# One evacuation for both halves of an attention block, in a fused attention and two-MLP kernel

## The chip, the core and the metric

The kernel runs on one core of a Trainium2 chip. The metric is the device time of one execution in microseconds. Before the change it is 1192.57 us, the median of three runs (1190.59 to 1194.06).

## The reference, cut to what matters

Three stages follow each other. The first is chunked attention: batch 4, 8 heads, 768 positions, head size 64. Each chunk of 32 queries sees 16 positions to its left, itself, 8 to its right, and 8 memory slots.

```python
for c in range(nc):
    scores = scale * np.matmul(q_c, k_full.transpose(0, 1, 3, 2))
    scores = scores - np.max(scores, axis=-1, keepdims=True)
    a = np.exp(scores)
    a = a / (np.sum(a, axis=-1, keepdims=True) + 1e-09)
    out[:, :, c_start:c_end] = np.matmul(a, v_full)
...
h = x @ w_in;  g = np.maximum(h, 0.0) + alpha * np.minimum(h, 0.0);  y = g @ w_out
h = y @ w_in;  g = h * (1.0 / (1.0 + np.exp(-1.702 * h)));           z = g @ w_out
```

The attention result, 3072 tokens by 512 channels, goes through a first MLP (hidden size 2048, leaky activation with a slope per channel) and a second one (gated by a sigmoid). The change lies in the last line of the attention loop: how the product with `v_full` leaves the accumulator.

## The kernel before, in words

The tokens are cut into 12 blocks of 256 (`TB`), numbered `nb`. A block's attention is done in two halves of 128 tokens. All products are made of pairs of 16-bit numbers: a float32 value is split into a rounded high part and a low remainder, and three products stand for one.

**Order of the work.** The first MLP is a loop of 96 steps of a block and a pair of hidden tiles (`order`, L970), 8 steps to a block. In a step `s` (L995) the TensorE does `mlp_g1` of block step `s - 4` (24 matmuls, L575) and later `mlp_g2` of an earlier one (24 matmuls, L655). The ScalarE and the VectorE do the activation (`mlp_act`, L610 and L613) and the split into high and low parts (`mlp_split`, by `cast_hi` L127 and `sub_lo` L130) between them. Three calls of `run_plan` in each step emit whatever else is due: attention of later blocks, the unpacking of weights, the preparation of the second MLP. A unit with time `t` is emitted by the first `run_plan` whose argument is over `t`; `run_plan(3 * s + 1)` stands behind `mlp_g1`, `run_plan(3 * s + 2)` ahead of `mlp_g2`, `run_plan(3 * s + 3)` behind it. The units of the blocks 3 to 11 come from the list `ATT` (L836), with `24 * nb + EX3 - 38` added, where `EX3` is 12; those of blocks 0 to 2 stand in the list `start` (L855). The order of emission is a priority: the kernel is built with `schedule_with_timeline_sim=True` (L1074), and an engine's final order can differ from it. Each engine then works through its own queue in order.

**The end of a block's attention.** For each half `i`, the normalised scores are split (`att_a16`, ScalarE L523, GpSimd L524) and transposed by a DMA that SyncE issues (`att_ta`, L530) into `aT`. `att_pv` (L533) then makes 48 small matmuls of 32 columns (L543: 4 pairs of heads, 4 chunks, 3 products) with the stationary tile `vbd`. Half 0 goes to the first bank of the accumulator tile `sps`, half 1 to the second:

```python
xp = sps[:, i].rearrange("p (j t) -> p j t", j=HP)
```

`sps` has three banks of 512 columns and one copy; the scores `q k` of every half (`att_qk`, L477 and L478) are written to the same tile. `att_xhi` (ScalarE, 512 columns, through L127) rounds a half to 16 bits into `xt`, and `att_xlo` (VectorE, 512 columns, through L130) writes the remainder. `xt` of a block is what its eight `mlp_g1` read.

By the list, the units of a block are emitted in this order: `att_pv` of half 0 at 32 behind the `mlp_g1` of a step; `att_xhi` of half 0 at 33 ahead of that step's `mlp_g2`; `att_xlo` of half 0 and `att_pv` of half 1 at 34 behind it; `att_xhi` and `att_xlo` of half 1 at 35 and 36, in the next step. Two steps after the first product the block's own `mlp_g1` begin. Blocks 0 and 1 use a version in 32 bits (`att_pv32`) with its own accumulator, and are not touched by the change except for a condition that falls away.

Of the kernel before, what the change touches and what calls it, by code (L numbers as in the profile page):

```python
# [26 lines left out]
F32B = (0, 1)  # L27
# [9 lines left out]
def kernel(  # L37
# [23 lines left out]
    HP = H // 2  # L61
# [7 lines left out]
    AS = 2.0 ** 14  # L69
# [56 lines left out]
    def cast_hi(hi, src, s):  # L126
        return nc.scalar.activation(out=hi, in_=src, func=ACTF.Copy, scale=s)  # L127

    def sub_lo(lo, hi, src, s):
        return nc.vector.scalar_tensor_tensor(out=lo, in0=src, scalar=s, in1=hi, op0=ALU.mult, op1=ALU.subtract)  # L130
# [142 lines left out]
    att = {}  # L273
# [8 lines left out]
    def bs(nb, i):  # L282
        return blk[nb][:, i:i + 1]
# [249 lines left out]
    def att_pv(nb, i):  # L533
        aT = att.pop(("a", nb, i))
        if i == 0:
            xt[nb] = xt_p.tile([128, 2, KT, TB], F16, tag="xt", name="xt")
        xp = sps[:, i].rearrange("p (j t) -> p j t", j=HP)
        for j in range(HP):
            for c in range(4):
                o = xp[:, j, 32 * c:32 * c + 32]  # L540
                w = vbd[:, 4 * i + c, j].rearrange("p a (d t) -> p (a d) t", t=2)
                for n, (wt, a) in enumerate(((0, 0), (1, 0), (0, 1))):
                    nc.tensor.matmul(out=o, lhsT=w[:, :, wt], rhs=aT[:, a, j, 32 * c:32 * c + 32], start=(n == 0), stop=(n == 2))  # L543
        att["xp", nb, i] = xp

    def att_xhi(nb, i):
        cast_hi(xt[nb][:, 0, :, i * 128:(i + 1) * 128], att["xp", nb, i], bs(nb, 9) if nb in F32B else 1.0 / AS)

    def att_xlo(nb, i):
        x = xt[nb][:, :, :, i * 128:(i + 1) * 128]  # L550
        sub_lo(x[:, 1], x[:, 0], att.pop(("xp", nb, i)), bs(nb, 9) if nb in F32B else 1.0 / AS)


    xt = {}
# [272 lines left out]
    def run_plan(t):  # L827
# [14 lines left out]
        (18, att_qk, 0), (18, att_ext, 0), (20, att_smax, 0), (21, att_qk, 1), (21, att_ext, 1),  # L842
        (22, att_exp, 0), (23, att_smax, 1), (24, att_sum, 0), (25, att_exp, 1), (26, att_a16, 0),
        (27, att_sum, 1), (28, att_ta, 0), (29, att_a16, 1), (31, att_ta, 1),
        (32, att_pv, 0), (33, att_xhi, 0), (34, att_xlo, 0), (34, att_pv, 1), (35, att_xhi, 1), (36, att_xlo, 1),
    ]
    for nb in range(3, NB):
        for u in ATT:
# [2 lines left out]
    def split(m, p):  # L851
# [16 lines left out]
        (-16.05, w_max, 1, 3), (-15.51, w_max, 0, 3), (-14.02, att_xmax, 0, 0), (-13.25, att_load, 2, 2),  # L868
        (-13.14, att_v32, 1, 0), (-12.97, w_all, 0, 2, 4), (-11.75, w_load, 0, 5), (-11.41, att_xall, 0),
        (-10.4, att_xs, 0), (-9.99, w_scale, 0, 2, 4), (-9.05, att_xhi, 0, 0), (-8.93, att_xlo, 0, 0),  # L870
        (-8.73, w_split_b, 0, 0), (-8.71, att_load, 2, 1), (-8.25, att_xhi, 0, 1), (-7.99, att_load, 2, 0),
        (-7.61, w_dec_a, 0, 2), (-7.5, w_dec_b, 0, 2), (-7.25, w_dec_b, 0, 1), (-7.2, w_load, 1, 5),
        (-6.9, w_max, 0, 4), (-6.52, att_max, 2, 0), (-6.51, att_xlo, 0, 1), (-5.97, w_max, 1, 1),
        (-5.96, att_qk32, 1, 0), (-4.67, w_split_a, 0, 1), (-4.66, w_max, 1, 0), (-3.68, att_max, 2, 2),
        (-2.76, att_max, 2, 1), (-2.32, w_dec_a, 0, 3), (-2.14, w_split_a, 0, 2), (-1.65, w_split_b, 0, 1),
# [22 lines left out]
        (25.09, att_vr, 2, 2), (25.62, w_split_b, 1, 0), (26.74, att_ta, 2, 0), (26.89, w_scale, 0, 6, 8),  # L898
        (27.59, att_a16, 2, 1), (28.18, w_load, 1, 4), (29.46, w_max, 1, 4), (29.5, w_split_a, 0, 4),
        (29.59, att_pv, 2, 0), (30.52, w_scale, 1, 4, 6), (30.65, att_ta, 2, 1), (31.18, w_dec_a, 0, 7),  # L900
        (31.7, w_split_b, 1, 2), (31.87, att_xhi, 2, 0), (32.19, att_pv, 2, 1), (33.03, w_dec_a, 0, 6),
        (33.15, w_split_b, 0, 4), (33.67, w_dec_b, 0, 7), (33.84, w_dec_b, 0, 6), (34.16, att_xhi, 2, 1),
        (34.77, w_split_a, 0, 6), (35.75, att_xlo, 2, 1), (35.88, att_xlo, 2, 0), (36.25, w_dec_b, 0, 5),
        (36.83, w_dec_a, 1, 4), (38.19, w_split_b, 0, 6), (38.37, w_dec_a, 1, 5), (39.13, w_split_a, 0, 5),
        (39.77, w_dec_b, 1, 4), (40.15, w_load, 1, 6), (40.17, w_max, 1, 6), (41.35, w_scale, 1, 6, 8),
        (42.12, w_dec_b, 1, 5), (42.5, w_part, 1), (42.81, w_split_a, 1, 5), (43.12, w_split_b, 0, 5),
# [7 lines left out]
    for g in range(NP):  # L914
        m, p = 2 + g % 2, g // 2
        t = 24 * (g + 3) - 8 + EX3
# [12 lines left out]
    for b in range(NB):  # L929
        t = 3 * ((NP * (b + 1) if b >= NA else HF * (NA + b + 1)) + L0) + 2 - 3  # L930
# [7 lines left out]
    for sb in range(NB // 2):  # L938
        t = Q0 + 48 * sb
# [3 lines left out]
        t = 48 * sb + 80 if sb else 101.5  # L943
# [3 lines left out]
        if sb == NB // 2 - 1:  # L947
            t = Q0 + 20
# [17 lines left out]
    sps = ps_s.tile([128, 3, 512], F32, name="sps")  # L966
# [56 lines left out]
    for q in range(STEPS // 2 + LQ):  # L1023
        t = Q0 + 6 * q
# [19 lines left out]
        if xs:  # L1044
            sb, p = divmod(q, NP)
# [33 lines left out]
```

## Time and profile before

| what | value |
| --- | --- |
| profiled execution, device time | 1190.76 us |
| its span, first to last instruction | 1189.0 us |
| runs | 1190.59, 1192.57, 1194.06 us |
| TensorE busy | 1078.8 us, 91% of the span |
| VectorE busy | 854.6 us, 72% |
| ScalarE busy | 632.8 us, 53% |
| GpSimd busy | 637.4 us, 54% |
| mean granted TensorE clock | 0.954 |

The first MLP with the attention and the weight work takes about the first 740 us, the second MLP the rest. Busy shares are means over the whole span. A time in a view is counted from the span's start. In a line of the timeline the first number is the start, the second the duration, the brackets hold the idle time before it and what ended that; an instruction that follows another closely may begin before the other has ended.

### The profile page before, as it was taken

The numbers are of one execution on the slowest core, as the hardware profiler recorded it, in microseconds if no ns is written. First come the engines' busy times: TensorE is split into PE (matmuls) and PEld (weight loads), VectorE is DVE, ScalarE is ACT, GpSimd is POOL, SyncE is SP. The second block draws the span as 40 slices with busy tenths as digits, with TensorE's granted clock in tenths as the row PEclk, the third lists the DMA queues.
The fourth block names the chain that finished last, engine by engine and source line by source line (L and its number), as shares of the span: only waits on it lengthen the run. The fifth ranks groups of instructions, "written<-read, shape, count | busy, mean of one in ns | idle before, by whom it ended". The sixth has DMA issues, their size and how long they took to land.

```text
span 1189.0 us, 25654 instructions
## 1 busy us (share of the span) xinstructions
PE 1078.8 (91%) x10294; PEld 956.7 (80%) x10294; DVE 854.6 (72%) x1509; ACT 632.8 (53%) x968; POOL 637.4 (54%) x740
## 2 busy tenths in 40 slices
PE   3676779988999887999899999989999999999998
PEld 3665668877888776887788988878888888888887
DVE  6898985659787777858698634787676767667662
ACT  4567555556766475756665632545444444443442
POOL 1244542318756456617562811787685676666672
PEclk8678889999899999999899999999999999999999
DMA  9969227576989678887965390640110202000001
GB/s 207 305 126 192 90 72 160 91 145 181 238 207 262 137 203 164 235 156 191 186 191 139 102 351 19 266 169 19 56 44 6 76 19 80 21 6 14 19 19 37
DMA packets 250536, 154.53 MB, mean 130 GB/s; under 512 B 201200, under 2 KB 221680, under 8 KB 249392
## 3 DMA queue, kind: packets, MB, share of 16 engines
q1 hardware_dynamic: 250416, 152.88, 50.3%
q8 instruction: 81, 1.33, 0.5%
q14 instruction: 39, 0.32, 0.1%
HBM read 91.96 MB, written 38.93 MB: 110 GB/s over the span
## 4 chain that ended last, share of the span: by engine, by line
PE 51%; DVE 19%; DMA 11%; POOL 5%; issue 5%; ACT 4%; SPq 4%; ACTq 0%; DVEq 0%; POOLq 0%
PE acc L669 17%; PE x L586 16%; PE h L575 8%; PE acc L655 8%; DVE g L130 3%; DVE gf L613 2%; DMA q<-q 2%; POOL ga L620 2%; DMA wbig<-in_moe_w_in_dram 2%; DVE wr L198 1%; DVE wmax L124 1%; DMA w<-in_moe_w_in_dram 1%; DVE wr L199 1%; DVE blk L124 1%; DMA vbd<-in_v_dram 1%
## 5 line engine op out<-in xcount | busy, mean ns | idle before, releaser
L620 POOL TENSOR_TENSOR ga<-ga 128x128 f32<-128x128 f32 x384 | 213.1, 579 | 170.7 <-DVE ga L618 158.6
L575 PE MATMUL h<-xt,wbig 128*128 128x256 f16 x2304 | 279.6, 279 | 22.8 <-ACT xt L127 17.0
L655 PE MATMUL acc<-g,wbig 128*128 128x256 f16 x2304 | 280.5, 280 | 8.9 <-DVE yf L685 4.0
L575 PEld LDWEIGHTS <-wbig 128*128 128x128 f16 x2304 | 230.4, 100 | 55.4 <-issue 24.5
L655 PEld LDWEIGHTS <-wbig 128*128 128x128 f16 x2304 | 229.7, 100 | 41.5 <-issue 8.9
L669 PE MATMUL acc<-w2o,g 128*128 128x256 f16 x2016 | 231.7, 274 | 4.0 <-ACT g L127 3.6
L586 PE MATMUL x<-yt,w2i 128*128 128x256 f16 x2016 | 229.9, 273 | 1.0 <-DVE ha L596 0.9
L669 PEld LDWEIGHTS <-g 128*128 128x128 f16 x2016 | 197.7, 98 | 28.9 <-ACT g L127 4.5
L586 PEld LDWEIGHTS <-w2i 128*128 128x128 f16 x2016 | 197.3, 98 | 24.2 <-issue 1.4
L130 DVE SCALAR_TENSOR_TENSOR g<-ga,gk,g 128x896 f16<-128x896 f32 x96 | 121.0, 1266 | 91.2 <-ACT g L127 90.9
L127 ACT ACTIVATE g<-ga,gk 128x896 f16<-128x896 f32 x96 | 99.0, 1038 | 96.0 <-POOL ga L620 87.0
L613 DVE SCALAR_TENSOR_TENSOR gf<-t,oma,h 128x256 f32<-128x256 f32 x192 | 83.5, 473 | 76.9 <-ACT t L610 76.9
L130 DVE SCALAR_TENSOR_TENSOR g<-gf,gk,g 128x512 f16<-128x512 f32 x81 | 80.5, 994 | 20.2 <-ACT g L127 20.0
L610 ACT ACTIVATE t<-h 128x512 f32<-128x512 f32 x96 | 56.7, 591 | 70.0 <-PE h L575 46.3
L803 POOL TENSOR_TENSOR o<-o 128x256 f32<-128x256 f32 x77 | 74.3, 979 | 10.0 <-ACT o L798 9.5
L617 ACT ACTIVATE ga<-ha,l2t 128x512 f32<-128x512 f32 x48 | 34.5, 718 | 80.7 <-DVE ha L598 80.7
L228 POOL TENSOR_TENSOR wt<-wr 128x512 f32<-128x512 f32 x16 | 24.0, 1499 | 81.1 <-DVE wr L205 81.0
L214 POOL TENSOR_TENSOR wbig<-wr,wbig 128x1024 f16<-128x1024 f32 x16 | 35.1, 2202 | 53.4 <-ACT wbig L209 53.4
L127 ACT ACTIVATE g<-gf,gk 128x512 f16<-128x512 f32 x81 | 57.7, 712 | 0.5 <-DVE gf L613 0.4
L494 ACT COPY sc<-sps 32x504 f32<-32x504 f32 (+2 forms) x112 | 56.2, 502 | 1.0
L618 DVE SCALAR_TENSOR_TENSOR ga<-ga,ha 128x512 f32<-128x512 f32 x48 | 35.6, 741 | 21.0 <-ACT ga L617 21.0
L543 PE MATMUL sps<-aT,vbd 128*128 128x32 f16 x960 | 27.5, 179 | 22.7 <-DVE xt L130 16.3
(194 smaller groups left out, 1514.7 us busy)
## 6 DMA issues: line engine op xcount, KB each, us to landing
yt_dr<-yh SPq DMA_DIRECT2D x42, 256.0 KB
yt<-yt_dr SPq DMA_DIRECT2D x42, 256.0 KB
w<-in_moe_w_in_dram SPq DMA_DIRECT2D x10, 1024.0 KB
w<-in_moe_w_out_dram SPq DMA_DIRECT2D x10, 1024.0 KB
vbd<-v_dr SPq DMA_DIRECT2D x80, 112.0 KB
w2i_dr<-wh SPq DMA_DIRECT2D x28, 256.0 KB
w2o_dr<-wh SPq DMA_DIRECT2D x28, 256.0 KB
w2i<-w2i_dr SPq DMA_DIRECT2D x4, 1792.0 KB
```

The source lines that it names most:

```text
L127: return nc.scalar.activation(out=hi, in_=src, func=ACTF.Copy, scale=s)
L130: return nc.vector.scalar_tensor_tensor(out=lo, in0=src, scalar=s, in1=hi, op0=ALU.mult, op1=ALU.subtract)
L494: nc.scalar.copy(d[32 * c:32 * c + 32, ..., 0:WIN], x[32 * c:32 * c + 32, ..., bo + CH * c:bo + CH * c + WIN])
L575: nc.tensor.matmul(out=hp[:, e], lhsT=w[:, wt, o:o + 128], rhs=x[:, xh, kk], start=(n == 0), stop=(n == 3 * KT - 1))
L586: nc.tensor.matmul(out=xs[bank][:, i], lhsT=w[:, o, wt, kk * 256 + c:kk * 256 + c + 128], rhs=yt[sb, yi][:, yh, kk], start=(n == 0), stop= ...
L610: nc.scalar.activation(out=t, in_=hp, func=ACTF.Relu, scale=-1.0)
L613: nc.vector.scalar_tensor_tensor(out=g[:, e], in0=t[:, e], scalar=oma[:, f:f + 1], in1=hp[:, e], op0=ALU.mult, op1=ALU.add)
L618: nc.vector.scalar_tensor_tensor(out=t, in0=t, scalar=1.0, in1=hp, op0=ALU.add, op1=ALU.mult)
L620: nc.gpsimd.tensor_tensor(out=g[:, out_], in0=g[:, x], in1=g[:, y], op=op)
L655: nc.tensor.matmul(out=acc[layer, b][dt // 2][:, dt % 2 * TB:(dt % 2 + 1) * TB], lhsT=w[:, wt, dt * 128:(dt + 1) * 128], rhs=g16[:, gh, e] ...
L669: nc.tensor.matmul(out=acc[layer, b][bank][:, i * 256:(i + 1) * 256], lhsT=g16[:, gh, gs], rhs=w[:, o, wt, p % 2], start=(p == 0 and n == ...
L803: e.tensor_tensor(out=ov[:, out_], in0=ov[:, x], in1=ov[:, y], op=op)
```

## The change

Both halves are multiplied first. The accumulator is laid out anew: a pair of heads now has 256 columns side by side, half 0 in the first 128, half 1 in the others, so that the two banks together hold the block's result in the order in which `xt` wants it. One ScalarE and one VectorE instruction of 1024 columns then take it out. In the list of the later blocks the second product is due at 33.5 and the evacuation at 34; in the list of the start the evacuation of block 2 is due at 35.75. `att_xhi` and `att_xlo` stay for blocks 0 and 1 alone.

```diff
-        xp = sps[:, i].rearrange("p (j t) -> p j t", j=HP)
+        xp = sps[:, 0:2].rearrange("p a (b t) -> p (a b) t", b=2)[:, :, i * 128:(i + 1) * 128]
...
-        att["xp", nb, i] = xp
+
+    def xp_both(nb):
+        return sps[:, 0:2].rearrange("p a n -> p (a n)"), xt[nb].rearrange("p a j t -> p a (j t)")
+
+    def att_x(nb):
+        xp, x = xp_both(nb)
+        cast_hi(x[:, 0], xp, 1.0 / AS)
+        sub_lo(x[:, 1], x[:, 0], xp, 1.0 / AS)
...
-        (32, att_pv, 0), (33, att_xhi, 0), (34, att_xlo, 0), (34, att_pv, 1), (35, att_xhi, 1), (36, att_xlo, 1),
+        (32, att_pv, 0), (33.5, att_pv, 1), (34, att_x),
...
-        (31.7, w_split_b, 1, 2), (31.87, att_xhi, 2, 0), (32.19, att_pv, 2, 1), (33.03, w_dec_a, 0, 6),
-        (33.15, w_split_b, 0, 4), (33.67, w_dec_b, 0, 7), (33.84, w_dec_b, 0, 6), (34.16, att_xhi, 2, 1),
-        (34.77, w_split_a, 0, 6), (35.75, att_xlo, 2, 1), (35.88, att_xlo, 2, 0), (36.25, w_dec_b, 0, 5),
+        (31.7, w_split_b, 1, 2), (32.19, att_pv, 2, 1), (33.03, w_dec_a, 0, 6),
+        (33.15, w_split_b, 0, 4), (33.67, w_dec_b, 0, 7), (33.84, w_dec_b, 0, 6),
+        (34.77, w_split_a, 0, 6), (35.75, att_x, 2), (36.25, w_dec_b, 0, 5),
```

## Rows read from the trace of the kernel before

**Rows 1.** Stretches: us, busy us (instructions) of PE, PEld, DVE, ACT, POOL, clock, DMA

```profile
233.00:673.00 440.00, 399.86 (x4200) 354.37 (x4197) 335.63 (x605) 273.37 (x430) 241.56 (x194) 0.96 0.78 184
```

**Rows 2.** Waits of the TensorE, 225 to 700 us: total, times, longest

```profile
PE sps L543 <- DVE xt L130: 16.3, 5, 4.1
PE sps L477 <- ACT sc L494: 7.2, 4, 2.4
PE sps L543 <- DMA aT<-a: 5.7, 2, 4.6
...
PE h L575 <- ACT xt L127: 3.7, 2, 2.1
```

**Rows 3.** Timelines of TensorE and VectorE, block 10

```profile
621.74 1.35 PE L543 MATMUL sps<-aT,vbd 128*128 128x32 f16 x48
...
629.56 1.44 PE L543 MATMUL sps<-aT,vbd 128*128 128x32 f16 x48 [2.63 <-DVE xt L130]
...
628.82 0.68 DVE L130 SCALAR_TENSOR_TENSOR xt<-sps,xt 128x512 f16<-128x512 f32 x1
```

**Rows 4.** Timelines of ScalarE and TensorE, block 7, its second half

```profile
473.32 1.48 ACT L326 ACTIVATE junk<-kf 128x1536 f16<-128x1536 f32 x1 [3.33 <-DMA kf<-in_mem_k_dram]
...
474.81 0.58 ACT L127 ACTIVATE xt<-sps 128x512 f16<-128x512 f32 x1
...
475.44 1.54 PE L575 MATMUL h<-xt,wbig 128*128 128x256 f16 x8 [2.12 <-ACT xt L127]
```

**Rows 5.** Stretches behind four of these waits, columns as in rows 1

```profile
465.80:470.00 4.20, 4.15 (x67) 3.49 (x67) 0.87 (x2) 3.78 (x5) 4.20 (x5) 0.62 1.24 180
...
475.40:481.50 6.10, 6.07 (x41) 4.80 (x41) 3.79 (x14) 5.46 (x9) 3.74 (x4) 0.72 1.09 270
...
576.20:581.50 5.30, 5.23 (x67) 4.04 (x67) 1.92 (x4) 3.82 (x5) 5.30 (x6) 0.50 1.12 203
...
629.50:633.40 3.90, 3.84 (x63) 3.22 (x63) 0.69 (x2) 0.60 (x1) 0.00 (x0) 0.57 0.73 135
```

**Rows 6.** Timelines of TensorE and of SyncE's transposes, blocks 4, 6 and 8

```profile
288.23 1.35 PE L543 MATMUL sps<-aT,vbd 128*128 128x32 f16 x48
...
296.10 1.23 SPq L530 DMA_TRANSPOSE aT<-a  x1
...
299.42 1.46 PE L543 MATMUL sps<-aT,vbd 128*128 128x32 f16 x48 [4.58 <-DMA aT<-a]
...
397.09 1.35 PE L543 MATMUL sps<-aT,vbd 128*128 128x32 f16 x48
...
401.80 1.29 SPq L530 DMA_TRANSPOSE aT<-a  x1
...
406.21 1.35 PE L543 MATMUL sps<-aT,vbd 128*128 128x32 f16 x48 [3.94 <-DVE xt L130]
...
511.43 1.35 PE L543 MATMUL sps<-aT,vbd 128*128 128x32 f16 x48
...
514.30 1.30 SPq L530 DMA_TRANSPOSE aT<-a  x1
...
517.73 1.37 PE L543 MATMUL sps<-aT,vbd 128*128 128x32 f16 x48 [1.12 <-DMA aT<-a]
```

**Rows 7.** Groups of ScalarE and VectorE, 225 to 700 us: busy, mean ns, idle before

```profile
L127 ACT ACTIVATE xt<-sps 128x512 f16<-128x512 f32 x18 | 10.6, 588 | 14.4 <-PE sps L543 14.4
...
L130 DVE SCALAR_TENSOR_TENSOR xt<-sps,xt 128x512 f16<-128x512 f32 x18 | 12.3, 686 | 19.5 <-ACT xt L127 19.5
```

**Rows 8.** The chain that ended last, 540 to 760 us: start, us, what

```profile
628.90 0.61 DVE xt L130
629.56 1.44 PE sps L543 x48
...
739.52 4.60 PE acc L655 x42
```

**Rows 9.** The same chain, 225 to 480 us, shares of the stretch

```profile
by line: issue 13.0%; DMA q<-q 6.4%; PE h L575 5.6%; DVE g L130 5.1%; DVE gf L613 4.6%; PE acc L655 3.4%; DMA w<-in_moe_w_in_dram 3.3%; DMA qf<-in_q_dram 3.2%; DVE blk L124 3.1%; DVE wmax L124 2.7%; DVE q L130 2.5%; ACT k L127 2.5%; DMA kf<
```

More of the change, by code (lines that the diff above doesn't have):

```diff
@@ L543, in att_pv @@
                     nc.tensor.matmul(out=o, lhsT=w[:, :, wt], rhs=aT[:, a, j, 32 * c:32 * c + 32], start=(n == 0), stop=(n == 2))
-        att["xp", nb, i] = xp
+    def xp_both(nb):
[4 more added lines that the diff above has]
+        sub_lo(x[:, 1], x[:, 0], xp, 1.0 / AS)
     def att_xhi(nb, i):
-        cast_hi(xt[nb][:, 0, :, i * 128:(i + 1) * 128], att["xp", nb, i], bs(nb, 9) if nb in F32B else 1.0 / AS)
+        cast_hi(xt[nb][:, 0, :, i * 128:(i + 1) * 128], att["xp", nb, i], bs(nb, 9))
     def att_xlo(nb, i):
         x = xt[nb][:, :, :, i * 128:(i + 1) * 128]
-        sub_lo(x[:, 1], x[:, 0], att.pop(("xp", nb, i)), bs(nb, 9) if nb in F32B else 1.0 / AS)
+        sub_lo(x[:, 1], x[:, 0], att.pop(("xp", nb, i)), bs(nb, 9))
     xt = {}
```

## The prediction, made before the changed kernel was run

> **What bounds the kernel now.** I looked first at the stretch that holds the blocks 3 to 11, since the edit touches nothing else but block 2. The TensorE is busy for 399.9 of its 440 us, the VectorE for 335.6, the ScalarE and the GpSimd for less [rows 1]: the TensorE is the fullest engine, and about 40 us of it lie idle. Next I asked what ended that idle time. The largest entry is the line that the change edits: five times the second product, L543, waits for the VectorE's remainder `xt` L130, 16.3 us in all [rows 2]. Only half 0 has been evacuated at that point, and half 1 goes to another bank, so no data call for this wait; it is there because both halves share the tile `sps`. The timeline of block 10 shows it from close by: half 0 is multiplied at 621.74, the TensorE goes on with other work, then stands for 2.63 us, up to 629.56, until the VectorE has read half 0 (628.82 + 0.68) [rows 3]. Then I followed the chain of waits, to see where such a wait sets the end. In block 10 it does: the chain goes from that `xt` into the second product [rows 8], and on through the TensorE alone to 744 us, where its last piece of the first MLP ends [rows 8]. Between 225 and 480 us the chain is mostly elsewhere: the two large matmul lines have 5.6% and 3.4% of it, transposes, loads, VectorE work and issue time the rest [rows 9].
>
> **The change part by part.** The sum is made against the profiled execution, 1190.76 us (span 1189.0). It is 1.81 us under the median of 1192.57; I give the time for the median.
>
> *The wait on the first half's evacuation goes.* The second product no longer follows a reader of `sps` from its own block. Of the 16.3 us [rows 2] I leave block 6's 3.94 in, because there its transposed `aT` comes hardly earlier (below) [rows 6]: 12.4 us of TensorE idle time go, in the blocks 5, 7, 9 and 10.
>
> *The late second evacuation goes.* In block 7 the first `mlp_g1` of the block waits 2.12 us for half 1's `xt`, which stood in the ScalarE's queue behind an instruction that waited 3.33 us for a load of the next block [rows 4]. Two such waits cost 3.7 us [rows 2]. The single evacuation is emitted a step earlier, ahead of that instruction, so I count them as gone.
>
> *The clock behind these waits.* After four of them the granted clock is 0.62, 0.72, 0.50 and 0.57 for 4.2, 6.1, 5.3 and 3.9 us [rows 5]. A stretch at mean clock c loses (1 - c) of its length: 1.6 + 1.7 + 2.7 + 1.7 = 7.6 us. If the waits go, so does this.
>
> *The second product comes earlier in its queue, and may meet its own DMA.* Now it is emitted ahead of the step's `mlp_g2`, not behind it. What is late next is `aT`. In block 4 the transpose is issued at 296.10 and the product starts at 299.42, 3.3 us on; in block 8 it is 3.4 us [rows 6]; for block 6, issued at 401.80, that makes an estimate of 405.2. If the second product stood directly behind the first, it would wait there from the first one's end: block 4 from 289.6 to 299.4, block 6 from 398.4 to 405.2, block 8 from 512.8 to 517.7. That is 9.8 + 6.8 + 4.9 = 21.5 us where 4.58 + 3.94 + 1.12 = 9.6 are waited now [rows 6], a loss of 11.9. If the builder keeps it where it stands, behind the `mlp_g2`, the loss is 0. These are the bounds; I take the middle, 6.0, since nothing in the trace tells the new place. In the other blocks `aT` was there, or the wait would be named for it.
>
> *The evacuation itself.* No row shows 1024 columns out of `sps`. A gain is bounded by the instruction that goes: ScalarE between 588 and 1176 ns, VectorE between 686 and 1372 ns [rows 7]; a cost above two of the old ones is excluded because no work is added. The elements are the same, so I take something near the upper end, some 0.1 us saved on each engine and block: 0 on the path. What covers it is the TensorE, busier than both. If that cover is gone, ten blocks give back 2 us at most.
>
> *The wait for both halves.* From the end of the second product to a finished `xt` it was 588 + 686 ns; it becomes at most 1176 + 1372, 1.3 us more. Behind the waiting ScalarE instruction stand the same step's activation L610 and, later, the rounding of the next block's `v`; behind the VectorE's stand L613 and the remainder of the `v` part. The ScalarE waits for `sps` now as well, 14.4 us in all, and the VectorE 19.5 us for the ScalarE's `xt` [rows 7]; these two waits become one of each per block. I count 0, because the block's own `mlp_g1` is emitted two steps after, and a step takes 7.0 us (511.43 less 288.23, for the 32 steps from block 4 to block 8 [rows 6]). Without that cover it costs ten times 1.3 us, 13 us.
>
> *The rest.* Matmuls, their order in a bank and the DMAs are the same in number; nothing moves past SyncE or GpSimd work. In block 2 the roundings move behind a weight rounding, while the remainders were the last to come; I take 0, within one of the old instructions, 0.7 us, either way [rows 7].
>
> **Sum.** On the TensorE's queue: 12.4 + 3.7 + 7.6 - 6.0 = 17.7 us. How much of it reaches the end? Certain places are where the chain passes: block 10, 2.63 + 1.7 = 4.3 us [rows 3, 5, 8]; and block 7's first `mlp_g1`, 2.12 + 1.7 = 3.8 us [rows 4, 5], less half of block 8's possible loss, (4.9 - 1.12) / 2 = 1.9 [rows 6]. That makes 6.2. Of the other 11.5 I give a sixth, 1.9, since the chain before is mostly not the TensorE's [rows 9]. Forecast: 8 us less, **1184.5 us**.
>
> A rule of the Trainium skill speaks against the edit: Perfetto Trace Analysis, section Optimizing Tensor Performance, asks that independent groups rotate through PSUM banks so that the evacuation of one overlaps the next group's matmuls. The trace agrees with the aim but shows that this overlap does not happen in five of the blocks, where the next group starts only when the evacuation is over [rows 2, 3]. By the rule the sum would be a loss, by the rows it is the gain above.
>
> **The rivals.**
>
> *Absorbed.* The waits go, but other queues hold the pace, and the TensorE waits elsewhere: for `sc` L494 before the scores, 7.2 us now [rows 2], or for `aT`. For it speaks the chain of 225 to 480 us [rows 9]; against it block 10, behind which the chain knows the TensorE alone [rows 8]. Time: 4.3 us of block 10 less a few: 1189 to 1196.
>
> *Slower: the product stands in front of its own transpose.* If the builder puts the second product directly behind the first, blocks 4, 6 and 8 lose the full 11.9 us, where the `mlp_g2` used to fill the time, and the ScalarE and VectorE stand behind one instruction each. Against block 10's 4.3 that is 7.6 us more: 1200.2. It decides if those 11.9 us lie on the path; from 4.3 us on the gain of block 10 is used up. The three late transposes speak for it, the idle time already spent there against it.
>
> *Slower: the lost overlap.* Evacuating both halves at the end makes `xt` late, and `mlp_g1` waits 1.3 us in each of ten blocks, 13 us less 4.3: 1201. It needs the first `mlp_g1` to be ready within 2.5 us of the second product; the two steps between speak against it. This is the mechanism by which the rule on rotating banks would win.
>
> *It does not do what it says.* The second product still waits for a reader of `sps`, such as the one of the block before: no change, 1192.6. That reader is done a block earlier, eight steps or 56 us.
>
> **How the numbers follow.** A measurement of this kernel can tell about 0.3%, 3.6 us, from no change. Forecast 0.58, absorbed 0.19, in front of its transpose 0.15, lost overlap 0.06, no effect 0.02. The forecast's own range is a gain of 3.6 to 17.7 us, 1175 to 1189. The range of 1174 to 1196 takes in the absorbed case and leaves out most of the slower ones. Faster: 0.58 and a little of the absorbed case, 0.60; same 0.23; slower 0.17.
>
> **What would show it.** Right: no L543 wait for `xt` L130, the two products nearer together, ten `xt` instructions of 1024 columns on each engine, the clock near 1 behind the products of the blocks 7, 9 and 10, the TensorE solid from 621 us on. The step on `aT` is wrong if its wait stays near 5.7 us or goes beyond 18 us. The forecast is wrong if these waits are gone and the first MLP ends as late as before, or if `sc` or `aT` waits have grown by as much.

## The result, and the profile after

The changed kernel takes **1205.83 us** (median of four runs, 1204.88 to 1206.51) against 1192.68 us for the kernel before in the same comparison: 1.0104 times, 95% interval [1.0085, 1.0123]. That is 13 us slower, where 8 us faster was forecast; it lies above the range.

The engines do the same work: the TensorE's busy time is 1082.7 us, 1078.8 before. From the page of the changed kernel, its first part:

```profile
PE 1082.7 (90%) x10294; PEld 958.7 (80%) x10294; DVE 851.8 (71%) x1499; ACT 631.9 (52%) x958; POOL 635.3 (53%) x740
```

The first product of block 11 starts at 687.74 us instead of 672.54. What follows is as long as before: 1204.2 - 687.74 = 516.5 and 1189.0 - 672.54 = 516.5. All of the loss is ahead of it. It is not all in one place: by the starts of the first products of the blocks 7, 8, 9, 10 and 11 the changed kernel is behind by 4.1, 8.2, 11.6, 10.0 and 15.2 us in the two profiled executions. In the changed kernel, lines past the edit carry a number 7 higher (L582 is the L575 of before, L617 the L610, L620 the L613, L662 the L655). The TensorE's waits between 225 and 715 us; the columns are those of [rows 2]:

```profile
PE sps L543 <- DMA aT<-a: 18.1, 3, 7.3
PE h L582 <- DVE gf L620: 7.8, 2, 4.4
PE sps L477 <- DMA vbd<-v_dr: 6.3, 1, 6.3
PE sps L477 <- ACT sc L494: 5.9, 2, 5.7
...
PE h L582 <- DVE xt L130: 0.7, 1, 0.7
...
PE h L582 <- ACT xt L127: 0.3, 1, 0.3
```

The edit did what it says. The wait of the second product for `xt`, 16.3 us in [rows 2], is gone, and the `mlp_g1`'s wait for the ScalarE's `xt` went from 3.7 to 0.3. Other waits came: `aT` from 5.7 to 18.1 us (4.58, 6.29 and 7.25 us in the blocks 4, 6 and 10), and 7.8 us in which an `mlp_g1` waits for the VectorE's half of the activation, `gf`, a wait that the kernel before doesn't have.

The new evacuation, from the view of the tile `xt`:

```profile
L127 ACT ACTIVATE xt<-sps x9: 1000/1019/1024, 237.3 to 691.9; 128x1024 f16<-128x1024 f32 x9
L130 DVE SCALAR_TENSOR_TENSOR xt<-sps,xt x9: 1203/1225/1226, 238.4 to 692.9; 128x1024 f16<-128x1024 f32 x9
```

1.02 us on the ScalarE and 1.23 us on the VectorE, a little less than two of the old ones [rows 7].

**Where the wait for `gf` comes from.** Block 7, timelines of the ScalarE, the VectorE and the TensorE of the changed kernel:

```profile
468.92 1.01 ACT L127 ACTIVATE xt<-sps 128x1024 f16<-128x1024 f32 x1
...
477.57 1.48 ACT L326 ACTIVATE junk<-kf 128x1536 f16<-128x1536 f32 x1 [4.88 <-DMA kf<-in_mem_k_dram]
...
479.05 0.58 ACT L617 ACTIVATE t<-h 128x512 f32<-128x512 f32 x1
479.53 2.05 ACT L127 ACTIVATE v<-vf,blk 128x1536 f16<-128x1536 f32 x1
...
479.66 0.87 DVE L620 SCALAR_TENSOR_TENSOR gf<-t,oma,h 128x256 f32<-128x256 f32 x2 [8.47 <-ACT t L617]
...
464.06 2.78 PE L582 MATMUL h<-xt,wbig 128*128 128x256 f16 x24
...
480.59 4.46 PE L582 MATMUL h<-xt,wbig 128*128 128x256 f16 x24 [4.38 <-DVE gf L620]
```

L326 takes the maximum over `k` of a later block (block 9) and waits for its load. The activation `t<-h` stands behind it: its input, the `mlp_g1` of 464.06, was finished at 466.84 (464.06 + 2.78), and the ScalarE is idle for the 4.88 us ahead of the maximum, yet the activation starts at 479.05. The VectorE then waits 8.47 us for `t`, and the TensorE 4.38 for `gf`. In the kernel before, the same queue had that step's activation and the rounding of `v` ahead of the maximum, and half 1's evacuation behind it. Its ScalarE timeline, block 7, ahead of the junk row of [rows 4]:

```profile
466.88 0.59 ACT L610 ACTIVATE t<-h 128x512 f32<-128x512 f32 x1
467.37 2.06 ACT L127 ACTIVATE v<-vf,blk 128x1536 f16<-128x1536 f32 x1
```

It is the same load that held up half 1's evacuation in [rows 4], there with 2.12 us of wait for the TensorE: the change took the evacuation out from behind it, and another instruction came to stand there.

So the change did not only move its own instructions. The builder, with other instructions to place, sorted the ScalarE's queue anew, and not that one alone: if the instructions of the two traces are matched by operation, tiles and sizes, at least 55 of 960 change their place in the ScalarE's queue, 90 of 1500 in the VectorE's and 28 of 740 in the GpSimd's. The activation was ready and stood, and the ScalarE did not look past the head of its queue. Perfetto Trace Analysis of the Trainium skill says the same in its section on the Tensor Engine Instruction: ScalarE and VectorE are strict FIFO. The rows agree. Block 9 repeats the pattern, with a wait of 3.43 us.

A third maximum, over `k` of block 10, is ahead of the rounding of `g` in the steps of block 8. Timelines of the ScalarE, the VectorE and the TensorE of the changed kernel:

```profile
538.76 1.48 ACT L326 ACTIVATE junk<-kf 128x1536 f16<-128x1536 f32 x1 [7.95 <-DMA qf<-in_q_dram]
...
540.24 0.70 ACT L127 ACTIVATE g<-gf,gk 128x512 f16<-128x512 f32 x1
...
548.49 2.32 ACT L494 COPY sc<-sps 32x504 f32<-32x504 f32 x4
...
540.98 0.75 DVE L130 SCALAR_TENSOR_TENSOR g<-gf,gk,g 128x512 f16<-128x512 f32 x1 [9.45 <-ACT g L127]
...
550.87 0.29 PE L477 MATMUL sps<-kt,q 128*128 128x160 f16 x1 [6.28 <-DMA vbd<-v_dr]
```

In the kernel before the rounding of `g` was ahead (ScalarE timeline, the maximum of block 10 being at 529.56):

```profile
523.03 0.71 ACT L127 ACTIVATE g<-gf,gk 128x512 f16<-128x512 f32 x1
```

The profile puts the TensorE's 6.28 us down to `vbd`, which these products don't read. They write to `sps`, and the ScalarE's copies of the scores out of `sps` end at 550.81 (548.49 + 2.32), just before they start. So this is likely a wait for `sc`.

**Where the late `aT` of block 10 comes from.** Timelines of GpSimd, ScalarE, SyncE and TensorE of the changed kernel:

```profile
629.01 1.49 POOL L518 TENSOR_TENSOR sc<-sc,rs 128x512 f32<-128x512 f32 x1
...
632.20 1.58 ACT L127 ACTIVATE k<-kf,blk 128x1536 f16<-128x1536 f32 x1 [4.72 <-DVE blk L112]
633.68 1.13 ACT L127 ACTIVATE q<-qf,blk 128x1024 f16<-128x1024 f32 x1
634.72 0.60 ACT L523 CAST a<-sc 128x512 f16<-128x512 f32 x1
...
637.04 1.29 SPq L530 DMA_TRANSPOSE aT<-a  x1
...
631.70 1.36 PE L543 MATMUL sps<-aT,vbd 128*128 128x32 f16 x48
640.31 1.44 PE L543 MATMUL sps<-aT,vbd 128*128 128x32 f16 x48 [7.25 <-DMA aT<-a]
```

The second half's scores were ready at 630.5 (629.01 + 1.49). Their rounding L523 stands behind the roundings of block 11's `k` and `q`, and that of `k` waits until 632.20 for its scale. So `a` comes 4.2 us late, the transpose is issued at 637.04, and the TensorE waits 7.25 us in front of the second product. In the kernel before, ScalarE timeline of block 10, the order was the other:

```profile
616.88 0.62 ACT L523 CAST a<-sc 128x512 f16<-128x512 f32 x1 [1.51 <-POOL sc L518]
620.31 1.58 ACT L127 ACTIVATE k<-kf,blk 128x1536 f16<-128x1536 f32 x1 [2.82 <-DVE blk L112]
```

The second half's rounding stands behind that of `k` in the blocks 4, 6 and 8 of the kernel before, the very blocks whose `aT` was late in [rows 6], and in 4, 6 and 10 of the changed one. Both places lie on the chain of waits; here for 470 to 486 us and for 630 to 645 us of the changed kernel:

```profile
472.77 4.78 DMA kf<-in_mem_k_dram
...
479.14 0.49 ACT t L617
...
479.66 0.87 DVE gf L620 x2
...
637.04 3.22 DMA aT<-a
...
640.31 1.44 PE sps L543 x48
```

**The clock.** Three stretches of the changed kernel, columns as in [rows 1]: behind block 7's products, behind its `gf` wait, behind block 10's second product:

```profile
459.00:463.00 4.00, 4.00 (x113) 3.82 (x112) 3.32 (x4) 2.78 (x4) 0.52 (x1) 1.00 0.10 25
480.50:485.00 4.50, 4.41 (x26) 3.34 (x27) 3.78 (x15) 4.50 (x8) 1.23 (x1) 0.62 0.15 53
640.30:644.20 3.90, 3.89 (x61) 3.14 (x61) 1.71 (x2) 1.02 (x1) 0.00 (x0) 0.50 0.66 119
```

Where a wait went, the clock is at 1.00; where a new one came, it falls to 0.62 and 0.50, as it did behind the old ones [rows 5]. 0.50 is the lower of the two levels, 1.2 GHz.

### The profile page after: what moved, and what is told of

It is laid out like the page before. It is cut to its first block, busy times and chain, and to the rows that moved or that the text cites. A ratio compares the mean times of both kernels' runs of the same rounds, so it can differ in the third digit from the quotient of the medians.

```text
span 1204.2 us, 25629 instructions
## 1 busy us (share of the span) xinstructions
PE 1082.7 (90%) x10294; PEld 958.7 (80%) x10294; DVE 851.8 (71%) x1499; ACT 631.9 (52%) x958; POOL 635.3 (53%) x740
## 4 chain that ended last, share of the span: by engine, by line
PE 53%; DVE 17%; DMA 11%; POOL 5%; issue 5%; SPq 4%; ACT 4%; ACTq 0%; DVEq 0%; POOLq 0%
PE acc L676 17%; PE x L593 16%; PE h L582 9%; PE acc L662 9%; DVE g L130 2%; DMA q<-q 2%; DVE gf L620 2%; POOL ga L627 2%; DVE wr L198 2%; DMA wbig<-in_moe_w_in_dram 1%; SPq L313 1%; DVE wmax L124 1%; DMA vbd<-v_dr 1%; DVE wr L199 1%; DMA vbd<-in_v_dram 1%
## 5 line engine op out<-in xcount | busy, mean ns | idle before, releaser
L582 PE MATMUL h<-xt,wbig 128*128 128x256 f16 x2304 | 279.4, 280 | 27.1 <-ACT xt L127 15.2
L662 PE MATMUL acc<-g,wbig 128*128 128x256 f16 x2304 | 280.5, 280 | 14.4 <-DVE yf L692 4.6
L582 PEld LDWEIGHTS <-wbig 128*128 128x128 f16 x2304 | 231.1, 100 | 60.6 <-issue 20.9
L662 PEld LDWEIGHTS <-wbig 128*128 128x128 f16 x2304 | 230.0, 101 | 48.0 <-issue 12.8
L620 DVE SCALAR_TENSOR_TENSOR gf<-t,oma,h 128x256 f32<-128x256 f32 x192 | 83.4, 472 | 91.7 <-ACT t L617 91.7
L130 DVE SCALAR_TENSOR_TENSOR g<-gf,gk,g 128x512 f16<-128x512 f32 x81 | 77.4, 956 | 27.8 <-ACT g L127 27.3
L617 ACT ACTIVATE t<-h 128x512 f32<-128x512 f32 x96 | 56.9, 593 | 75.9 <-PE h L582 52.4
L239 POOL TENSOR_TENSOR wh<-wt,wh 128x512 f16<-128x512 f32 x32 | 43.6, 1368 | 8.9 <-ACT wh L238 8.8
```

Source lines behind the costliest of these rows:

```text
L239: nc.gpsimd.tensor_tensor(out=hv[:, 1], in0=src, in1=hv[:, 0], op=ALU.subtract)
L582: nc.tensor.matmul(out=hp[:, e], lhsT=w[:, wt, o:o + 128], rhs=x[:, xh, kk], start=(n == 0), stop=(n == 3 * KT - 1))
L617: nc.scalar.activation(out=t, in_=hp, func=ACTF.Relu, scale=-1.0)
L620: nc.vector.scalar_tensor_tensor(out=g[:, e], in0=t[:, e], scalar=oma[:, f:f + 1], in1=hp[:, e], op0=ALU.mult, op1=ALU.add)
L662: nc.tensor.matmul(out=acc[layer, b][dt // 2][:, dt % 2 * TB:(dt % 2 + 1) * TB], lhsT=w[:, wt, dt * 128:(dt + 1) * 128], rhs=g16[:, gh, e] ...
```

## The experiments

Three theories stood at the start. **A**: the second product now stands in front of its own late transpose. **B**: the ScalarE's queue has the maximum, with its wait for a load, ahead of activations, in the blocks 7 and 9. **C**: the wide instructions, or the later evacuation, cost it. A hold, below, is a call that pins an instruction in its engine's queue behind the one emitted just before it; the kernel before has it already on the roundings of `v`. Ratios are to the kernel before, with their 95% intervals. Kernels with a hold on the maxima have their lines two further down (L545 for L543).

| run | kernel and edit | median us | ratio |
| --- | --- | --- | --- |
| e1 | changed, second product at 34 | 1203.05 | 1.0088 [1.0064, 1.0113] |
| e2 | before, new order, narrow evacuations | 1204.31 | 1.0104 [1.0081, 1.0128] |
| e3 | changed, all later maxima held | 1184.41 | 0.9936 [0.9912, 0.9959] |
| e5 | before, all later maxima held | 1188.68 | 0.9965 [0.9950, 0.9980] |
| e8 | e2, all later maxima held | 1187.34 | 0.9951 [0.9936, 0.9966] |
| e9 | e3, maxima emitted earlier | 1186.00 | 0.9937 [0.9916, 0.9958] |
| e6 | changed, maximum over `k` of two blocks held | 1201.97 | 1.0071 [1.0045, 1.0097] |
| e10 | before, those two maxima early | 1199.25 | 1.0052 [1.0034, 1.0070] |
| e11 | changed, rounding of `k` held | 1201.73 | 1.0071 [1.0052, 1.0090] |
| e12 | e6 and e11 together | 1195.83 | 1.0025 [1.0009, 1.0041] |
| e13 | before, rounding of `k` held | 1193.80 | 1.0009 [0.9993, 1.0025] |
| e14 | changed, all maxima and `k` held | 1188.09 | 0.9961 [0.9938, 0.9983] |
| e15 | e12, second product at 34 | 1197.28 | 1.0025 [1.0008, 1.0042] |
| e16 | before, all maxima and `k` held | 1189.94 | 0.9979 [0.9963, 0.9995] |
| e17 | e3, second product at 34 | 1186.10 | 0.9942 [0.9921, 0.9962] |
| e18 | e12, and `q` held behind `k` | 1189.05 | 0.9957 [0.9940, 0.9973] |
| e20 | before, `k` and `q` held | 1189.56 | 0.9965 [0.9947, 0.9983] |
| e19 | changed, all maxima, `k` and `q` held | 1185.06 | 0.9923 [0.9898, 0.9947] |

**The wide instructions, or the order?** The run e2 has the old layout and four evacuations of 512 columns, in the changed kernel's order; e1 is the changed kernel with the second product behind the `mlp_g2`.

```diff
# e1, from the changed kernel
-        (32, att_pv, 0), (33.5, att_pv, 1), (34, att_x),
+        (32, att_pv, 0), (34, att_pv, 1), (34, att_x),
# e2, from the kernel before
-        (32, att_pv, 0), (33, att_xhi, 0), (34, att_xlo, 0), (34, att_pv, 1), (35, att_xhi, 1), (36, att_xlo, 1),
+        (32, att_pv, 0), (33.5, att_pv, 1), (34, att_xhi, 0), (34, att_xhi, 1), (34, att_xlo, 0), (34, att_xlo, 1),
```

> The changed kernel with the second product due at 34 again, so that it stands behind the step's mlp_g2 in the TensorE's queue (2.6 us later); all else as changed. Theory A (the second product stands in front of its own transpose; its waits for aT grew from 5.7 to 18.1 us): the waits of blocks 6 and 10 shrink by 2.6 us each, to about 13 us in all, and the time falls by 4 to 8 us, to 1198 to 1202. Theory B (the ScalarE's queue: the maximum over the next k, which waits for a load, now stands ahead of activations in blocks 7 and 9): no more than 2 us from 1205.8, since that order is the same here.

> The kernel before, with the second product moved up to 33.5 as in the change, and the four old evacuations of 512 columns behind it, in the old layout. Theories A and B both: the time of the changed kernel within 3 us, 1203 to 1209, since both come from the order of the work. Theory C (the wide instructions of 1024 columns and the later evacuation of half 0 cost the time): back to 1190 to 1195.

Measured: e2 loses the same without one evacuation of 1024 columns, and shows the same waits for `aT` and `gf`. So the wide instructions are not the loss. The later evacuation, the other half of C, is in e2 as well, and e2 can't rule it out; e3 and e18 below can, since they keep it and lose nothing. The TensorE waits of e2, 225 to 715 us:

```profile
PE sps L543 <- DMA aT<-a: 18.6, 3, 7.2
PE sps L477 <- ACT sc L494: 11.3, 3, 6.2
PE h L575 <- DVE gf L613: 8.3, 2, 4.9
```

e1 got back at most 3 us (its interval overlaps that of the changed kernel), though its `aT` waits fell from 18.1 to 13.5, as theory A had it, which had wanted 1198 to 1202 us with them. The product's place alone is not the loss.

**The maxima in order.**

```diff
# e3 from the changed kernel, e5 from the kernel before, e8 from e2
-            nc.scalar.activation(out=z[:, 0:n], in_=t, func=ACTF.Abs, accum_out=bs(nb, i))
+            x = nc.scalar.activation(out=z[:, 0:n], in_=t, func=ACTF.Abs, accum_out=bs(nb, i))
+            if nb > 2:
+                tc.keep_in_program_order(x)
```

> The changed kernel with the maximum over q and k (ScalarE, L326) of blocks 3 to 11 held in the order of emission, so that it can't stand ahead of activations that are emitted before it. Theory B: the TensorE's waits for the activation of h (gf, 7.8 us) and those behind it go, 5 to 10 us faster, 1196 to 1201. Theory A: waits for aT stay near 18 us and the time within 3 us of 1205.8.

> The kernel before with the same hold on the maximum: what the hold does by itself. Theory B: it has that order in fewer places there, so 0 to 4 us faster than 1192.7. Theory A: no change, within 3 us.

> The kernel before with both products first, four evacuations of 512 columns behind them, and the hold on the maxima of blocks 3 to 11. If the gain under the hold (1184.4 against 1188.7) comes from the order of the products: 1182 to 1187. If it comes from the wide instructions: 1187 to 1191.

Measured: the hold takes 21 us off the changed kernel and 4 off the kernel before, and turns a loss of 13 us into a gain. The TensorE's waits of e3, 225 to 715 us:

```profile
PE mx L119 <- ACT junk L326: 21.6, 7, 6.1
PE sps L479 <- ACT sc L496: 11.2, 4, 4.4
PE sps L545 <- DMA aT<-a: 2.5, 3, 1.6
```

The waits for `gf` are gone, but so, nearly, are those for `aT`, which the hold was not aimed at: a hold re-sorts more than the instruction it pins. The gain is twice what theory B had expected at most. So e3, with e5 beside it, shows that the order is the cause, not which part of it. And the maxima, now last, are waited for themselves (21.6 us). e8 came out at 1187.3, between e3 and e5, and its interval overlaps both: it doesn't tell the order of the products from the wide instructions. To emit the maxima earlier did not help:

```diff
# e9, from e3
-        (0, att_max, 1), (1, att_max, 0), (1, att_max, 2), (2, att_all, 0, 3), (4, att_scale, 0, 3),
+        (-6, att_max, 1), (-5, att_max, 0), (1, att_max, 2), (2, att_all, 0, 3), (4, att_scale, 0, 3),
```

> The changed kernel with the hold, and the maxima of k and q emitted at -6 and -5 in place of 0 and 1, since under the hold the TensorE waited 21.6 us for them before the small matmuls of the scale. Theory B: these waits shrink and the time falls by 3 to 12 us from 1184.4; if the loads land too late for the new place, the ScalarE waits for them again and it is slower than 1184.4.

Measured: 1186.0, no gain over e3, though the TensorE no longer waits for the maxima.

**B alone, taken away and put in.** e6 holds only the maximum over `k` of the blocks 9 and 11, those that had moved ahead in the blocks 7 and 9. e10 forces them ahead in the kernel before.

```diff
# e6, from the changed kernel: as e3, but
+            if nb in (9, 11) and i == 1:
# e10, from the kernel before: the hold of e6, and
-            at(24 * nb + EX3 - 38 + u[0], u[1], nb, *u[2:])
+            t = u[0]
+            if nb in (9, 11) and u[1] in (att_load, att_max) and u[2] == 1:
+                t = -13.7 if u[1] is att_load else -13.6
+            at(24 * nb + EX3 - 38 + t, u[1], nb, *u[2:])
```

> The changed kernel with the maximum over k held in the order of emission for blocks 9 and 11 alone, the two whose maximum the change moved ahead of an activation of block 7 and block 9; all other maxima as in the changed kernel. Theory B (those two places cost the time): at least 6 us back, 1192 to 1199. Theory A (the second product in front of its transpose, 18 us of waits for aT): within 3 us of 1205.8.

> The kernel before, products and evacuations untouched, with the load and the maximum over k of blocks 9 and 11 emitted so that the maximum stands ahead of the activation and of the rounding of v after the first evacuation of blocks 7 and 9, as it does in the changed kernel. Theory B: slower by 5 to 12 us, 1197 to 1204, with waits of the TensorE for gf behind them. Theory A: within 3 us of 1192.4.

Measured: e6 gives back 3.9 us, less than the 6 that theory B had asked for; the `gf` waits of `mlp_g1` are gone, but those for `aT` rose from 18.1 to 23.7 us. e10 costs the kernel before 6.5 us, with the order of the changed kernel in block 7 again, the activation directly behind the maximum (ScalarE timeline of e10):

```profile
473.88 1.48 ACT L326 ACTIVATE junk<-kf 128x1536 f16<-128x1536 f32 x1 [4.13 <-DMA kf<-in_mem_k_dram]
...
475.36 0.58 ACT L612 ACTIVATE t<-h 128x512 f32<-128x512 f32 x1
```

But the waits of `mlp_g1` for `gf`, which theory B had expected, did not come in e10. The VectorE waits 7.40 us for that activation; the TensorE waits longer for `xt` instead, 20.7 us in front of the second product (16.3 before) and 5.9 in front of `mlp_g1` (3.7 before). So a maximum forced ahead costs time, and holding it gives time back; that the two maxima are worth all of the 3.9 or 6.5 us is not shown, since both runs moved other instructions too. Where the time is lost is told below.

**The second half's rounding behind `k`.**

```diff
# e11 from the changed kernel, e13 from the kernel before; e12 with the hold of e6, e14 and e16 with that of e3
-        if i == 2 and nb > 2:
+        if i in (1, 2) and nb > 2:
             tc.keep_in_program_order(x)
```

> The changed kernel with the rounding of k (ScalarE, L127) held in the order of emission, so that the rounding of the second half's scores, which leads to its transpose, stands ahead of it in every block; the maxima are left as in the change. Theory A (the second product in front of a late transpose): its waits for aT fall from 18 us to under 6 us and the time by 4 to 9 us, 1197 to 1202. Theory B: the place of the maxima is unchanged, so within 3 us of 1205.8.

> The changed kernel with both: the rounding of k held in every block, the maximum over k held in blocks 9 and 11. Theories A and B together: both losses go, 1188 to 1195, about the kernel before or under it. If one of them has no part in it, the time stays with the other's single run (1202 for the maxima).

> The kernel before with the hold on the rounding of k: the control. Theory A: its own waits for aT (5.7 us) go, 0 to 6 us faster than 1192.7; the waits for the first evacuation stay, or grow.

> The changed kernel with the maxima over q and k and the rounding of k all held from block 3 on. Theory A: the hold on the maxima alone left 2.5 us of waits for aT, so 0 to 3 us faster than 1184.4; Theory B: no more than 2 us either way.

Measured: e11 gives back 4.1 us, but its waits for `aT` stay at 12.6 us, not under 6 as expected, with 7.3 us in block 10 still. e12 with both holds gives back 10.0, a little more than the two apart (8.0) and a little less than expected. The same hold gains the kernel before nothing (e13). With the maxima held it gains nothing more (e14: 3.7 us over e3, with overlapping intervals). 3 us of the loss were left.

**The rest.** First guess: the second product's place, with the diff of e1 on e12 (e15) and on e3 (e17). e16 is the kernel before with the holds of e14.

> The changed kernel with the two holds of the earlier run together (rounding of k, and the maximum over k of the blocks 9 and 11), and the second product due at 34 instead of 33.5, behind the step's mlp_g2. The two holds alone measured 1195.8, 3.0 above the kernel before. If what is left of the loss is the second product's place ahead of the mlp_g2, in front of a transpose that is not there yet (waits for aT were 15.7 us with the two holds), this run gives back about 3 us: 1192 to 1194, with aT waits near 10 us. If the rest lies elsewhere (the scores' waits for sc, 19.6 us there against 7.2 in the kernel before): no gain, 1195 to 1197.

> The kernel before with both holds on the ScalarE's queue (all later maxima and the rounding of k in program order). It is the fourth corner: the changed kernel with the same holds measured 1188.1 and with the maxima alone 1184.4, the kernel before with the maxima alone 1188.7. If the order of the queue is what the change lost by, and the change itself gains what the wait for xt costs, this is slower than the changed kernel by 2 to 5 us: 1190 to 1193. If the change itself is worth nothing once the order is held: 1187 to 1189.

> The best version so far (the changed kernel, maxima in program order, 1184.4) with the second product due at 34, behind the step's mlp_g2. Its aT waits were 2.5 us in all. If the place of the product still costs something there: 1182 to 1184. If it costs nothing, or the later evacuation takes it back: 1184 to 1187.

Measured: e15 and e17 gain nothing, though in e15 the waits for `aT` fell from 15.7 to 9.5 us, and e16 gains 3 us on the kernel before. The product's place is not it, and a smaller total of `aT` waits is not by itself a shorter time. The rows of e12 told more; block 10, timelines of ScalarE and TensorE:

```profile
622.12 1.15 ACT L127 ACTIVATE q<-qf,blk 128x1024 f16<-128x1024 f32 x1 [4.85 <-DVE blk L112]
623.17 0.60 ACT L525 CAST a<-sc 128x512 f16<-128x512 f32 x1
623.68 1.57 ACT L127 ACTIVATE k<-kf,blk 128x1536 f16<-128x1536 f32 x1
...
630.27 1.44 PE L545 MATMUL sps<-aT,vbd 128*128 128x32 f16 x48 [5.74 <-DMA aT<-a]
```

`k` is held, and `q` has taken its place: it waits for the same scale, and the half's rounding stands behind it as before. So in e18 `q` is emitted directly behind `k` and held too; e20 is the same in the kernel before, e19 in e14.

```diff
-        if i in (1, 2) and nb > 2:
+        if nb > 2:
...
-        (5, att_hi, 1), (6, att_lo, 1), (6, att_hi, 0), (8, att_tk), (7, att_lo, 0), (9, att_tq),
+        (5, att_hi, 1), (5, att_hi, 0), (6, att_lo, 1), (8, att_tk), (7, att_lo, 0), (9, att_tq),
```

> The changed kernel with the two holds (rounding of k, maximum over k of blocks 9 and 11), and now the rounding of q as well: it is emitted directly behind that of k and held there. In the run with the two holds the rounding of q had taken k's place in the blocks 4, 8 and 10: in block 10 it waits 4.85 us and the rounding of the second half's scores stands behind it, and the product waits 5.74 us for aT. If that is the rest of the loss, this run comes back to the kernel before or a little under it: 1191 to 1194, with aT waits under 6 us. If the rest lies elsewhere: 1195 to 1197.

> The kernel before with the same order of a, k and q (both held behind the second half's rounding). With k alone held it measured 1193.8. If a late aT costs the kernel before something too (blocks 4, 6 and 8), it gains up to 2 us: 1190 to 1192. If the wait for xt stands there in any case: 1192 to 1195.

> The changed kernel with all later maxima held and k and q behind the second half's rounding. The maxima alone held gave 1184.4 with aT waits of 2.5 us, maxima and k 1188.1. If a late aT is what is left: 1183 to 1186. If the maxima held cost as much by their own waits for loads as the rest gains: 1186 to 1189.

Measured: e18 gives back all 13 us and 3 to 4 more. Its block 10, the same timelines, and its waits for `aT`, 225 to 715 us:

```profile
620.27 0.62 ACT L525 CAST a<-sc 128x512 f16<-128x512 f32 x1 [2.28 <-POOL sc L520]
623.83 1.58 ACT L127 ACTIVATE k<-kf,blk 128x1536 f16<-128x1536 f32 x1 [2.93 <-DVE blk L112]
...
625.61 1.35 PE L545 MATMUL sps<-aT,vbd 128*128 128x32 f16 x48 [0.81 <-DMA aT<-a]
...
PE sps L545 <- DMA aT<-a: 5.4, 4, 2.4
```

e20, the control, gains 3.1 us on the kernel before, a little more than expected, and has no wait for `aT` left. e19 is at 1185.1, as expected if a late `aT` was what was left, but no faster than e3.

**Where the loss falls.** The table counts from the start of a block's first product to that of the next, in us, in the one profiled execution of each run; plus is slower. One execution differs from the next, so a single entry is an estimate.

| run, against | up to block 7 | 7 to 8 | 8 to 9 | 9 to 10 | 10 to 11 |
| --- | --- | --- | --- | --- | --- |
| changed, before | +4.1 | +4.1 | +3.4 | -1.6 | +5.2 |
| e2, before | +2.7 | +2.5 | +4.5 | -1.6 | +4.9 |
| e10, before | +2.8 | +2.5 | +1.0 | -0.4 | +2.0 |
| e6, changed | -0.6 | -3.1 | -1.1 | +2.0 | -1.3 |
| e11, changed | -3.4 | +0.3 | -0.1 | 0.0 | -0.1 |
| e12, changed | -4.5 | -3.8 | -1.5 | +0.8 | -1.6 |
| e18, changed | -3.3 | -3.2 | -2.9 | +1.0 | -8.1 |

The maximum in block 7 costs some 3 us: 2.5 where it is forced ahead (e10), 3.1 to 3.8 back where it is held (e6, e12, e18), nothing where it is left (e11). The one in block 9 looks the same and costs nothing; why the two differ is open. The place of the second half's rounding costs some 3 us ahead of block 7, which e11 gives back, and more in block 10, where `q` takes the place of `k` in e11 and e12, and only e18 gives the time back. Between the blocks 8 and 9, the third maximum stands ahead of the rounding of `g` in e2 and e11 too, and the loss is there too; in e6, e12 and e18 that rounding is ahead again, and 1.1 to 2.9 us come back. No run holds this maximum alone.

**What the change is worth by itself.** With the ScalarE's order held in the same way in both kernels, the changed one is ahead each time: 1184.4 against 1188.7 (all maxima, e3 and e5), 1188.1 against 1189.9 (with `k`, e14 and e16), 1189.1 against 1189.6 (`k` and `q`, e18 and e20, of which only e18 has two maxima held as well). That is 0.5 to 4 us; the intervals of each pair overlap, so only the direction is likely, not a size. The edit's loss of 13 us, however, is gone in all three pairs. The best versions are the changed kernel with the holds of e3 or e19, 0.6 to 0.8% under the kernel before; they can't be told from each other, nor from e9 and e17.

## Why the prediction was wrong

- **The wait for `xt`** (12.4 us to go): right, and block 6's as well, 16.3 us to nothing. There the wait for `aT`, 6.29 us, stands in its place. That the old wait came from the shared tile was argued, not tried.
- **The late second evacuation** (3.7 us): right for `xt`, of which 0.3 us of wait for the ScalarE's part are left and 0.7 for the VectorE's. But the term took the cause for gone with it. The load (of block 9, two blocks on, not of the next one) holds the ScalarE's queue as before, and block 7's next `mlp_g1` waits 4.38 us by way of the activation where 2.12 us went.
- **The evacuation itself** (0.1 us saved on each engine): right in size, 2 x 588 - 1019 = 157 ns and 2 x 686 - 1225 = 147 ns.
- **The wait for both halves** (0): right. The rival of the lost overlap had 13 us of waits of `mlp_g1` for `xt`; the changed kernel has 1.0 us of them, and e18 keeps the late evacuation and loses nothing. Perfetto Trace Analysis of the Trainium skill, section Optimizing Tensor Performance, wants groups to rotate through banks; the loss that the prediction had ascribed to the rule, an `mlp_g1` that waits for a late `xt`, is that 1.0 us here.
- **The clock behind the waits** (7.6 us): right for the waits that went, but new waits lowered it elsewhere, to 0.62 and 0.50.
- **The second product and its DMA** (a loss of 6.0, between 0 and 11.9 us): the waits of the slower rival did come. Waits for `aT` grew by 12.4 us, 18.1 less 5.7. That the total is near the rival's 11.9 is luck: block 4's wait is 4.58 us as before, and block 8 has none. The estimate took the transposes of [rows 6] as late by nature, in the blocks 4, 6 and 8. They were late by the ScalarE's order (e20, which changes that order in the kernel before, has no such wait), and after the change it was block 10, where the gain of 4.3 us had been held certain, that waited 7.25 us. With the order held (e18) the stretch from block 10 to 11 is 2.9 us shorter than in the kernel before. Moving the product back (e1, e15) does not undo the loss.
- **"The rest"** is the step that failed: "nothing moves past SyncE or GpSimd work", the prediction says, and it counts nothing for a new order of any queue. It allowed for an order of the builder's own only in the place of the second product. The queues were sorted anew, and that cost what the change had gained and 13 us more: the same edit takes 1189.1 and 1184.4 us with pins on the ScalarE's instructions (e18, where the rounding of `q` is also emitted earlier, and e3), with the kernel before at 1189.6 and 1188.7 under like pins (e20, e5). The inversions in the ScalarE's queue, each of one ready instruction behind one that waits, are where the time is seen to go. The prediction's 8 us gain needed an unchanged order around the edit; with a held order the measured difference is 0.5 to 4 us in its direction, not clear of the noise.

Left open: how the 13 us split between the inversions beyond the estimates of the table (each hold shifts others, in the queues of the VectorE and GpSimd too), and the place of the third maximum, in the steps of block 8, which was not tried alone.

## What to carry to other kernels

Where a scheduler places instructions by simulated times, an edit to one engine's list can re-sort other queues, so compare each engine's final order before and after, and look for a ready instruction that now stands behind one that waits for a load. Price a moved step by who ends up behind whom, not by its own duration. A tuned order that only the scheduler produced is worth pinning before an edit: here pins on ScalarE instructions took some 3 to 4 us off the kernel before (e5, e16, e20; e13's took nothing off), about as much as the edit is worth under the same pins.

## What the runs showed that was not expected

Of the hardware little: one instruction of 1024 columns reads two banks in 1.02 us on the ScalarE and 1.23 on the VectorE. The surprise was the reach of the queue's order: a maximum of 1.48 us that waits 4.88 us for its load, ahead of a ready activation of 0.58 us, stood at the head of a chain in which the VectorE waited 8.47 us and the TensorE 4.38 us, with the granted clock at 0.62 behind it. The same pattern in block 9, with waits of 8.01 and 3.43 us, cost nothing against the kernel before: a wait seen in one trace is not yet a loss.
